# Head mixing on pieces of the TensorE array: four quarter products in place of one full product and three single-pass ones

## The chip, the cores and the metric

The kernel runs on one core of a Trainium2 chip. The metric is the device time of one execution in microseconds (us), lower is better. Before the change it is 1879.54 us, the median of 3 runs (1875.44 to 1880.68).

## The reference

```python
scores = (q @ k.T) / sqrt(64)                        # 8 batches, 12 heads, 448 tokens, head size 64
scores = einsum('bhij,hg->bgij', scores, w_pre)      # heads mixed before the softmax ("premix")
attn   = softmax(scores, axis=-1)                    # 1e-9 added to the sum
attn   = einsum('bhij,hg->bgij', attn, w_post)       # heads mixed after it ("mix")
x      = (attn @ v) as 3584 tokens x 768             # "values"
h      = x @ w_in                                    # 768 -> 2048
out    = (h - tanh(h)) @ w_out                       # 2048 -> 768
```

All inputs and the output are float32.

## The kernel before

The program has two stages on the time axis: attention up to about 931 us, then the feed-forward part, whose code the change leaves alone. In attention a batch's 448 query tokens are cut into blocks of 120, 120, 120 and 88. For a block, `scores` forms the products of two heads at a time on the two row halves of TensorE's array (fp32r, three products to each, line 475) and copies each head's 120x448 result from PSUM into the tile `s` (line 481, on ScalarE or VectorE).

To mix heads, 12 heads must lie on the partitions. So `gather` (line 496) moves, by a DMA from SBUF to SBUF, the 12 heads of ten tokens into one tile `t` of 120 partitions x 448 keys. A block has 12 (or 9) such groups of ten tokens, and the program's loop takes two groups at a place: 180 places in all. At place p:

1. `gather` of the two groups of place p+2, on SP's queue, and behind them up to six loads and stores that earlier places put into a list (`issue(6)`). Tiles of even groups have three buffers, those of odd groups two.
2. `premix(p)`: the even group in one float32 product with the block-diagonal 120x120 `wpre` (line 512); the odd group in three fp32r products (lines 515 to 517) from parts `th` and `tl` of its tile, which `split` made a place earlier on VectorE (line 504) and GpSimd (line 505).
3. `norm(p-1)`: reciprocals of the softmax sums, and `wpost` scaled by them into `wr` on ScalarE (line 545).
4. `expo(p)`: the row maximum on VectorE (line 527), exp with its sum on ScalarE (line 529).
5. What a plan puts into this place: `scores` of four heads of a later block, or half of the `values` of an earlier one (line 598, float32, on the two column halves of the array), transposes of q or k, loads.
6. `mix(p-1)`: for each group four float32 products of 112 keys each, with `e` as stationary operand and `wr` (120 columns) as moving one, into one PSUM tile `ps_o` with a single buffer (line 557). Its copy to `at` on ScalarE (line 566) is issued at the start of the next place.

Scores of heads 2hp and 2hp+1 go to ScalarE and VectorE for even hp, and both to ScalarE for odd hp, so three of four copies are ScalarE's. In the places beyond the fourth, steps of a conversion of the feed-forward weights (lines 80 to 104) are spread over VectorE, ScalarE and GpSimd.

The order on PE, ScalarE, VectorE, GpSimd and SP is the order of the code (`in_order`), so a waiting instruction holds what stands behind it on its engine. The loads of a batch's keys (`load_k`, three tiles of four heads, two buffers) are planned from the first place of the batch's predecessor's second block, less one, and their transposes (`prep_k`) two places after each load or later.

Of the kernel before, what the change touches and what calls it, by code (L numbers as in the profile page):

```python
# [148 lines left out]
def kernel_body(  # L149
# [21 lines left out]
    GP = GI * H  # L171
    starts = list(range(0, S, MT))
# [164 lines left out]
    with ExitStack() as st:  # L337
# [127 lines left out]
        def scores(i, hp, engines=None):  # L465

            b, m = blocks[i]
            n = sizes[m]
            if hp == 0:
                sts[i] = sp.tile([MT, H, S], F32, name="s", tag="s")  # L470
            (qh, ql), (kh, kl) = qbs[i], kks[b, hp // 2]
            pss = [ps_m.tile([P, 512], F32, name="ps_q", tag="ps_m") for _ in halves]
            for x, (qx, kx) in enumerate(((qh, kh), (qh, kl), (ql, kh))):
                for a, ps in zip(halves, pss):
                    nc.tensor.matmul(ps[:n, :S], qx[a, hp, :], kx[a, hp % 2], start=(x == 0), stop=(x == 2))  # L475

            def rest():

                two = engines or (nc.scalar.copy, nc.scalar.copy if hp % 2 else nc.vector.tensor_copy)
                for j, (eng, ps) in enumerate(zip(two, pss)):  # L480
                    eng(sts[i][:n, 2 * hp + j, :], ps[:n, :S])

            sooner.append(rest)
# [7 lines left out]
        tg, ts, te = {}, {}, {}  # L491

        def gather(t, eng=nc.sync):
            i, g = groups[t]
            x = gp.tile([GP, S], F32, name="t", tag=f"t{t % 2}", bufs=3 - t % 2)
            eng.dma_start(x[: rows[t], :], sts[i][tokens[t].start : tokens[t].stop : tokens[t].step])
            tg[t] = x

        def split(t, eng=nc.gpsimd):
            n = rows[t]  # L500
            x = tg.pop(t)
            th = gp.tile([GP, S], F32R, name="th", tag="th", bufs=2)
            tl = gp.tile([GP, S], F32R, name="tl", tag="tl", bufs=2)
            nc.vector.tensor_copy(th[:n, :], x[:n, :])  # L504
            eng.tensor_sub(tl[:n, :], x[:n, :], raw(th[:n, :]))  # L505
            ts[t] = (th, tl)

        def premix(p):

            pa, pb = [ps_p.tile([P, S], F32, name="ps_p", tag="ps_p") for _ in range(2)]  # L510
            n = rows[2 * p]
            nc.tensor.matmul(pa[:n, :], wpre[:n, :n], tg.pop(2 * p)[:n, :], start=True, stop=True)  # L512
            n = rows[2 * p + 1]
            th, tl = ts.pop(2 * p + 1)
            nc.tensor.matmul(pb[:n, :], wph[:n, :n], th[:n, :], start=True, stop=False)
            nc.tensor.matmul(pb[:n, :], wpl[:n, :n], th[:n, :], start=False, stop=False)
            nc.tensor.matmul(pb[:n, :], wph[:n, :n], tl[:n, :], start=False, stop=True)  # L517
            return pa, pb

        def expo(p, pss):  # L520
            zs = gp.tile([GP, 3, 2], F32, name="zs", tag="zs")
            es = []
            for j, ps in enumerate(pss):
                n = rows[2 * p + j]

                mx = gp.tile([GP, 1], F32, name="mx", tag="mx")
                nc.vector.tensor_reduce(out=mx[:n, :], in_=ps[:n, :], axis=AX.X, op=ALU.max, negate=True)  # L527
                e = gp.tile([GP, S], F32, name="e", tag="e", bufs=4)
                nc.scalar.activation(  # L529
                    e[:n, :], ps[:n, :], AF.Exp, bias=mx[:n, :], scale=1.0, accum_out=zs[:n, 0, j : j + 1]  # L530
                )
# [3 lines left out]
        def norm(p):  # L535
            zs = te[p][1]
            wr = gp.tile([GP, 2, P], F32, name="wr", tag="wr", bufs=2)[:, :, :GP]
            n0, n1 = rows[2 * p], rows[2 * p + 1]
            for j, n in enumerate((n0, n1)):

                nc.vector.tensor_scalar_add(zs[:n, 1, j : j + 1], zs[:n, 0, j : j + 1], 1e-9)
            for js, n in ((slice(0, 2), n0),) if n0 == n1 else ((slice(0, 1), n0), (slice(1, 2), n1)):
                nc.vector.reciprocal(zs[:n, 2, js], zs[:n, 1, js])
            for j, n in enumerate((n0, n1)):
                nc.scalar.mul(wr[:n, j, :], wpost[:n, :], zs[:n, 2, j : j + 1])  # L545
            te[p].append(wr)

        def mix(p):
            es, _, wr = te.pop(p)
            ps = ps_o.tile([P, 2, 512], F32, name="ps_o", tag="ps_o")  # L550
            for j, e in enumerate(es):
                i, g = groups[2 * p + j]
                n = rows[2 * p + j]
                if g == 0:
                    ats[i] = kp.tile([CP, NC, H, MT], F32, name="at", tag="at", bufs=2)
                for c in range(NC):
                    nc.tensor.matmul(  # L557
                        ps[:CP, j, c * GP : (c + 1) * GP], e[:n, c * CP : (c + 1) * CP], wr[:n, j, :],
                        start=True, stop=True,
                    )  # L560
# [90 lines left out]
        tmp_w = kp.tile([P, 2 * GP + 2 * H], F32, name="tmp_w", tag="at", bufs=2)  # L651
        w12 = tmp_w[:H, 2 * GP : 2 * GP + 2 * H].rearrange("p (w h) -> p w h", w=2)
# [11 lines left out]
        def scores_of(i, hq):  # L664
# [10 lines left out]
        repeat = tmp_w[:H, GP : 2 * GP]  # L675
        nc.gpsimd.memset(repeat, 0.0)
        nc.gpsimd.affine_select(
            out=repeat.rearrange("p (i h) -> p i h", i=GI), in_=repeat.rearrange("p (i h) -> p i h", i=GI),
            compare_op=ALU.not_equal, fill=1.0, base=0, pattern=[[0, GI], [-1, H]], channel_multiplier=1,
        )  # L680
        ps_w = bank()[:GP, : 2 * H].rearrange("p (w g) -> p w g", w=2)
        nc.tensor.matmul(ps_w.rearrange("p w g -> p (w g)"), repeat, w12.rearrange("p w g -> p (w g)"), start=True, stop=True)
        wpre, wpost = [cst.tile([GP, P], F32, name=x)[:, :GP] for x in ("wpre", "wpost")]
        pre_v = wpre.rearrange("p (i g) -> p i g", i=GI)
        post_v = wpost.rearrange("p (g i) -> p g i", i=GI)
        nc.vector.tensor_copy(pre_v, ps_w[:, 0, :].unsqueeze(1).to_broadcast([GP, GI, H]))
        nc.vector.tensor_copy(post_v, ps_w[:, 1, :].unsqueeze(2).to_broadcast([GP, H, GI]))
        for x, step in ((pre_v, [[H, GI], [0, H]]), (post_v, [[0, H], [H, GI]])):

            nc.gpsimd.affine_select(  # L690
                out=x, in_=x, compare_op=ALU.is_ge, fill=0.0, base=0, pattern=[[-a, n] for a, n in step],
                channel_multiplier=1,
            )
            nc.gpsimd.affine_select(
                out=x, in_=x, compare_op=ALU.is_ge, fill=0.0, base=H - 1, pattern=step, channel_multiplier=-1,
            )
# [23 lines left out]
        wph, wpl = [cst.tile([GP, P], F32R, name=x)[:, :GP] for x in ("wph", "wpl")]  # L720
        nc.vector.tensor_copy(wph, wpre)
        nc.vector.tensor_sub(wpl, wpre, raw(wph))
# [6 lines left out]
        split(1, nc.vector)  # L729
# [54 lines left out]
        for b in range(1, B):  # L784
            p, o, done = first[blocks.index((b - 1, 1))] // 2 - 1, 0, []
            for hq in range(3):
# [4 lines left out]
                o = max(p + 2, o + 1)  # L791
# [26 lines left out]
        for p in range(NPL + 3):  # L818
# [18 lines left out]
            if p + 1 < NPL:  # L837
                split(2 * p + 3)
# [97 lines left out]
```

## Time and profile before

| what | value |
|---|---|
| median of 3 runs | 1879.54 us |
| the profiled execution's own time | 1880.95 us |
| its span, first to last instruction | 1879.2 us |
| time outside the span | 1.75 us |
| mean granted TensorE clock | 0.998 |
| GpSimd busy | 451.9 us (24%) |
| line 505 (`tl`) on GpSimd | x179, 204.4 us |
| line 504 (`th`) on VectorE | x180, 82.4 us |
| line 545 (`wr`) on ScalarE | x360, 123.8 us |

A float32 product appears in the trace as two records of the same line, an fp32r product as one. A row of the timeline merges neighbours of the same line on one engine; its second number runs from the first start to the last end. PE's ends are modelled, so the starts of neighbours tell the rate.

### The profile page before, as it was taken

How to read it: one execution, taken by the hardware profiler on the slowest of the kernel's cores; microseconds unless marked ns; L12 is line 12 of the kernel's file. 1: busy time of each engine (PE TensorE's matmuls, PEld its weight loads, DVE VectorE, ACT ScalarE, POOL GpSimd, SP SyncE). 2: the span in 40 equal slices, each digit the busy share in tenths (PEclk: the TensorE clock that was granted, in tenths of full speed). 3: DMA queues.
4: the chain of work that ended last, by engine and by line, in shares of the span. 5: the costliest groups of instructions: out<-in, count | busy, mean ns of one | idle time of the engine just before them, and what ended most of it. 6: DMA issues, size and time to landing. Idle time of an engine off the chain costs nothing.

```text
span 1879.2 us, 35344 instructions
## 1 busy us (share of the span) xinstructions
PE 1851.1 (99%) x13150; PEld 1525.9 (81%) x13150; DVE 1184.7 (63%) x2457; ACT 1133.8 (60%) x2503; POOL 451.9 (24%) x401
## 2 busy tenths in 40 slices
PE   8999999999999999999999999999999999999998
PEld 6777887787878777877788888888888888888887
DVE  5676766767776676766456556556566566565555
ACT  5787887878888788788634443434434434433433
POOL 2344444444444345444201000000000000000000
PEclk9999999999999999999999999999999999999999
DMA  6667658676675757656565565665655655655651
GB/s 162 183 183 201 189 166 221 182 208 190 177 216 171 209 177 205 195 164 189 212 255 193 206 246 192 223 218 196 235 213 196 235 205 196 237 209 191 233 193 42
DMA packets 232795, 371.92 MB, mean 198 GB/s; under 512 B 98992, under 2 KB 207536, under 8 KB 218288
## 3 DMA queue, kind: packets, MB, share of 16 engines
q1 hardware_dynamic: 231740, 368.45, 60.5%
q8 instruction: 104, 1.70, 0.4%
q10 hardware_dynamic: 884, 1.22, 0.2%
q14 instruction: 67, 0.55, 0.1%
HBM read 245.37 MB, written 47.19 MB: 156 GB/s over the span
## 4 chain that ended last, share of the span: by engine, by line
PE 86%; DMA 6%; ACT 3%; DVE 2%; issue 2%; POOL 1%; SPq 0%; ACTq 0%; POOLq 0%; DVEq 0%
PE ps_o L557 13%; PE ps_h L256 8%; PE ps_h L260 8%; PE ps_h L255 8%; PE ps_m L598 7%; PE ps_p L512 6%; PE ps_q L475 6%; PE ya L303 5%; PE ya L300 5%; PE ya L301 5%; DMA t<-s 4%; PE yb L303 3%; PE yb L301 3%; PE yb L300 3%; PE ps_p L517 2%
## 5 line engine op out<-in xcount | busy, mean ns | idle before, releaser
L557 PEld LDWEIGHTS ps_o<-wr,e 120*112 120x112 f32 (+1 forms) x2880 | 307.2, 177 | 49.8 <-issue 30.1
L557 PE MATMUL ps_o<-wr,e 120*112 120x120 f32 (+1 forms) x2880 | 340.5, 271 | 4.1 <-ACT wr L545 4.1
L527 DVE TENSOR_REDUCE mx<-ps_p 120x1 f32<-120x448 f32 x360 | 218.6, 622 | 136.9 <-PE ps_p L512 136.7
L505 POOL TENSOR_TENSOR tl<-t,th 120x448 fp32r<-120x448 f32 x179 | 204.4, 1142 | 391.8 <-DVE th L504 221.5
L287 ACT CAST gh<-r 128x512 fp32r<-128x512 f32 x112 | 69.6, 621 | 373.3 <-DVE r L280 373.3
L256 PE MATMUL ps_h<-xl,w 128*128 128x512 f32 x672 | 263.2, 392 | 0.5 <-POOL pad L222 0.5
L255 PE MATMUL ps_h<-xh,w 128*128 128x512 f32 x672 | 262.8, 391 | 0.0
L529 ACT ACTIVATE e<-ps_p,mx 120x448 f32<-120x448 f32 x360 | 225.8, 636 | 36.7 <-DVE mx L527 36.1
L245 POOL TENSOR_TENSOR xl<-rx,xh 128x512 fp32r<-128x512 f32 x38 | 53.7, 1415 | 741.3 <-ACT xh L244 741.3
L566 ACT COPY at<-ps_o 112x960 f32<-112x960 f32 x156 | 154.5, 990 | 113.4 <-PE ps_o L557 112.5
L303 PE MATMUL ya<-w,gl 128*128 128x512 f32 x448 | 177.1, 395 | 0.7 <-DVE gl L288 0.7
L276 DVE SCALAR_TENSOR_TENSOR r<-qa,ps_h 128x512 f32<-128x512 f32 x112 | 77.0, 687 | 158.7 <-ACT t L273 158.7
L300 PE MATMUL ya<-w,gh 128*128 128x512 f32 x448 | 175.0, 391 | 1.3 <-ACT gh L287 1.3
L301 PE MATMUL ya<-w,gh 128*128 128x512 f32 x448 | 174.9, 390 | 0.0
L260 PE MATMUL ps_h<-xh,w 128*128 128x512 f32 x672 | 170.5, 389 | 0.0
L512 PE MATMUL ps_p<-t,wpre 120*120 120x448 f32 x360 | 165.7, 542 | 4.3 <-ACT e L529 3.5
L598 PE MATMUL ps_m<-at,vr 112*64 112x120 f32 (+1 forms) x3072 | 163.3, 263 | 1.9 <-ACT at L566 1.5
L598 PEld LDWEIGHTS ps_m<-at,vr 112*64 112x64 f32 x3072 | 149.7, 138 | 14.7 <-ACT at L566 3.7
L270 ACT ACTIVATE u<-ps_h 128x512 f32<-128x512 f32 x112 | 66.9, 597 | 149.2 <-PE ps_h L260 149.2
L260 PEld LDWEIGHTS ps_h<-xh,w 128*128 128x128 f32 x672 | 126.1, 188 | 26.2
L256 PEld LDWEIGHTS ps_h<-xl,w 128*128 128x128 f32 x672 | 126.6, 188 | 24.6 <-POOL pad L222 0.9
L255 PEld LDWEIGHTS ps_h<-xh,w 128*128 128x128 f32 x672 | 126.6, 188 | 22.9
(102 smaller groups left out, 3622.0 us busy)
## 6 DMA issues: line engine op xcount, KB each, us to landing
w<-ws SPq DMA_DIRECT2D x112, 1536.0 KB
t<-s SPq DMA_DIRECT2D x342, 210.0 KB
cr<-in_moe_w_in_dram SPq DMA_DIRECT2D x24, 512.0 KB
cr<-in_moe_w_out_dram SPq DMA_DIRECT2D x32, 384.0 KB
vr<-in_v_dram SPq DMA_DIRECT2D x24, 448.0 KB
kr<-in_k_dram SPq DMA_DIRECT2D x23, 448.0 KB
out_dram<-ob SPq DMA_DIRECT2D x24, 384.0 KB
qr<-in_q_dram SPq DMA_DIRECT2D x23, 360.0 KB
```

The lines of the kernel that those rows point to most:

```text
L255: nc.tensor.matmul(ph, wh[:, fs], xh, start=(c == 0), stop=False)
L256: nc.tensor.matmul(ph, wh[:, fs], xl, start=False, stop=False)
L260: nc.tensor.matmul(ph, wl[:, fs], xh, start=False, stop=(c == NK - 1))
L300: nc.tensor.matmul(y, gh[:, tok], wh[:, es], start=first, stop=False)
L301: nc.tensor.matmul(y, gh[:, tok], wl[:, es], start=False, stop=False)
L303: nc.tensor.matmul(y, gl[:, tok], wh[:, es], start=False, stop=last)
L505: eng.tensor_sub(tl[:n, :], x[:n, :], raw(th[:n, :]))
L512: nc.tensor.matmul(pa[:n, :], wpre[:n, :n], tg.pop(2 * p)[:n, :], start=True, stop=True)
L527: nc.vector.tensor_reduce(out=mx[:n, :], in_=ps[:n, :], axis=AX.X, op=ALU.max, negate=True)
L529: nc.scalar.activation(e[:n, :], ps[:n, :], AF.Exp, bias=mx[:n, :], scale=1.0, accum_out=zs[:n, 0, j : j + 1])
L557: nc.tensor.matmul(ps[:CP, j, c * GP : (c + 1) * GP], e[:n, c * CP : (c + 1) * CP], wr[:n, j, :], start=True, stop=True,)
L598: nc.tensor.matmul(pv[j * D : (j + 1) * D, r, :n], vt[:, j, c, :], ats[i][:, c, 2 * hp + j, :n], start=(c == 0), stop=(c == NC - 1),)
```

## The change

- `gather` moves a group in two DMAs of five tokens each (60 partitions): five tokens to partitions 0 to 59, the others to partitions 64 and up.
- `premix` makes four float32 products: group j and token half r, rows 64r and up of the array, columns 64j and up. Both groups' first halves land in one PSUM tile, both second halves in the other. `split`, `wph` and `wpl` are gone.
- `expo` and `norm` work on 128 partitions; `wr` has 60 columns in place of 120.
- `mix` makes 16 float32 products of 60 rows x 112 columns with 60 moving columns in place of 8 of 120 rows with 120 columns; group j lies on row half j, and the two alternate.
- of four score copies two go to ScalarE and two to VectorE.
- keys are loaded three places earlier, and transposed at the earliest four places after the load in place of two.

```diff
-        def split(t, eng=nc.gpsimd):
...
         def gather(t, eng=nc.sync):
             i, g = groups[t]
-            x = gp.tile([GP, S], F32, name="t", tag=f"t{t % 2}", bufs=3 - t % 2)
-            eng.dma_start(x[: rows[t], :], sts[i][tokens[t].start : tokens[t].stop : tokens[t].step])
+            x = gp.tile([P, S], F32, name="t", tag=f"t{t % 2}", bufs=3 - t % 2)
+            tok, n = tokens[t], half_rows(t)
+            src = lambda u: sts[i][u[0] : u[-1] + 1 : u.step]
+            for a, u in zip(halves, (tok[:GH], tok[GH:])):
+                eng.dma_start(x[a.start : a.start + H * len(u), :], src(u))
...
         def premix(p):
-            nc.tensor.matmul(pa[:n, :], wpre[:n, :n], tg.pop(2 * p)[:n, :], start=True, stop=True)
...
-            nc.tensor.matmul(pb[:n, :], wph[:n, :n], th[:n, :], start=True, stop=False)
-            nc.tensor.matmul(pb[:n, :], wpl[:n, :n], th[:n, :], start=False, stop=False)
-            nc.tensor.matmul(pb[:n, :], wph[:n, :n], tl[:n, :], start=False, stop=True)
+            for j, to in enumerate(halves):
+                for r, (a, ps) in enumerate(zip(halves, pss)):
+                    k = slice(a.start, a.start + H * half_rows(2 * p + j)[r])
+                    nc.tensor.matmul(ps[to, :], wpre[k, :], ts[j][k, :], start=True, stop=True)
...
         def mix(p):
-                for c in range(NC):
-                    nc.tensor.matmul(
-                        ps[:CP, j, c * GP : (c + 1) * GP], e[:n, c * CP : (c + 1) * CP], wr[:n, j, :],
+            for r, e in enumerate(es):
+                for c in range(NC):
+                    for j, a in enumerate(halves):
+                        k = slice(a.start, a.start + H * half_rows(2 * p + j)[r])
+                        nc.tensor.matmul(
+                            ps[:CP, j, c * GP : (c + 1) * GP].rearrange("p (h i) -> p h i", i=GI)[:, :, r * GH : (r + 1) * GH],
+                            e[k, c * CP : (c + 1) * CP], wr[k, r, :],
...
-                two = engines or (nc.scalar.copy, nc.scalar.copy if hp % 2 else nc.vector.tensor_copy)
+                two = engines or (nc.scalar.copy, nc.vector.tensor_copy)
...
-            p, o, done = first[blocks.index((b - 1, 1))] // 2 - 1, 0, []
+            p, o, done = first[blocks.index((b - 1, 1))] // 2 - 4, 0, []
...
-                o = max(p + 2, o + 1)
+                o = max(p + 4, o + 1)
```

The order on PE, before, over a place with scores and the mix ahead of it (`ps_o` is mix, `ps_p` premix, `ps_q` scores):

```order
L557 MATMUL ps_o<-wr,e 112x120 x8
L512 MATMUL ps_p<-t,wpre 120x448
L515 MATMUL ps_p<-th,wph 120x448
L516 MATMUL ps_p<-th,wpl 120x448
L517 MATMUL ps_p<-tl,wph 120x448
L475 MATMUL ps_q<-kk,qh 88x448 x4
L475 MATMUL ps_q<-kk,ql 88x448 x2
L475 MATMUL ps_q<-kk,qh 88x448 x4
L475 MATMUL ps_q<-kk,ql 88x448 x2
L557 MATMUL ps_o<-wr,e 112x120 x8
```

The same place on PE, now:

```order
L554 MATMUL ps_o<-wr,e 112x12x5 x16
L516 MATMUL ps_p<-t,wpre 64x448 x4
L477 MATMUL ps_q<-kk,qh 88x448 x4
L477 MATMUL ps_q<-kk,ql 88x448 x2
L477 MATMUL ps_q<-kk,qh 88x448 x4
L477 MATMUL ps_q<-kk,ql 88x448 x2
L554 MATMUL ps_o<-wr,e 112x12x5 x16
```

Nothing changes places on PE: four products stand where four stood, sixteen where eight stood.

SP's queue at a batch's end, before (`t<-s` is a gather, `kr` keys, `vr` values, `xs` the attention's result, `cr` and `ws` the weight conversion):

```order
L367 DMA xs_57<-x 768x1x208
L496 DMA t<-s 120x1x448 x2
L367 DMA qr<-in_q_dram 88x12x64
L367 DMA vr<-in_v_dram 112x4x256
L367 DMA kr<-in_k_dram 112x16x64
L367 DMA ws_65<-cs 128x384
L367 DMA ws_65<-cl 128x384
L496 DMA t<-s 120x1x448 x2
L367 DMA vr<-in_v_dram 112x4x256
L367 DMA kr<-in_k_dram 112x16x64
```

and now:

```order
L505 DMA t<-s 60x1x448 x8
L369 DMA kr<-in_k_dram 112x16x64
L369 DMA ws_65<-cs 512x1x128
L369 DMA ws_65<-cl 512x1x128
L505 DMA t<-s 60x1x448 x4
L369 DMA kr<-in_k_dram 112x16x64
L369 DMA cr<-in_moe_w_out_dram 128x768
L505 DMA t<-s 60x1x448 x4
L369 DMA vr<-in_v_dram 112x4x256
L369 DMA xs_57<-x 768x1x208
L505 DMA t<-s 60x1x448 x4
```

The first two loads of keys moved ahead of the store of `xs` and away from the loads of values, and each place has four gathers.

What the gathers of two places wait for on SP, before (`PE` and `Pool` are those engines' use of the buffer that the gather overwrites, `DMAHW` an earlier transfer that must have landed):

```order
L496 DMA t<-s 120x1x448 [waits DMAHW2_49,PE_49]
L496 DMA t<-s 120x1x448 [waits DMAHW3_49,Pool_49]
L367 DMA kr<-in_k_dram 112x16x64 [waits DMAHW4_49]
L496 DMA t<-s 120x1x448 [waits DMAHW5_49,PE_49]
L496 DMA t<-s 120x1x448 [waits DMAHW6_49,DMAHW0_49,Pool_49]
```

and now:

```order
L505 DMA t<-s 60x1x448 [waits DMAHW4_49,DVE_49,Activation_49]
L505 DMA t<-s 60x1x448 [waits DMAHW5_49]
L505 DMA t<-s 60x1x448 [waits DMAHW6_49,PE_49]
L505 DMA t<-s 60x1x448 [waits DMAHW7_49]
L369 DMA kr<-in_k_dram 112x16x64 [waits DMAHW0_49]
L505 DMA t<-s 60x1x448 [waits DMAHW1_49]
L505 DMA t<-s 60x1x448 [waits DMAHW2_49]
L505 DMA t<-s 60x1x448 [waits DMAHW3_49,PE_49]
```

The odd group's gather waited for GpSimd, which a place earlier had made `tl` from that buffer; it now waits for PE, that is for the premix of its own place.

More of the change, by code (lines that the diff above doesn't have):

```diff
@@ L673, in kernel_body @@
         flush()
[L675 removed]
+        repeat = tmp_w[:H, :P]
         nc.gpsimd.memset(repeat, 0.0)
[L677 to L681, printed above, removed]
[L682 removed]
@@ L683, in kernel_body @@
[L683 to L696, printed above, removed]
+        for a in halves:
+            nc.gpsimd.affine_select(
+                out=repeat[:, a][:, :HP].rearrange("p (i h) -> p i h", i=GH),
+                in_=repeat[:, a][:, :HP].rearrange("p (i h) -> p i h", i=GH),
+                compare_op=ALU.not_equal, fill=1.0, base=0, pattern=[[0, GH], [-1, H]], channel_multiplier=1,
+            )
@@ L699, in kernel_body @@
+        for w, x in enumerate((wpre, wpost)):
+            nc.gpsimd.memset(x[:, HP:], 0.0)
+            nc.vector.tensor_add(x[:, :HP], both[:, w, 0], both[:, w, 1])
         busy(3, ps_b)
```

88 lines of the change are left out of this document (46 added, 42 removed).

## The prediction

> **What bounds the kernel now.** I read the page first, then the engines' busy time over the steady part of attention.
>
> ```profile
> PE 1851.1 (99%) x13150; PEld 1525.9 (81%) x13150; DVE 1184.7 (63%) x2457; ACT 1133.8 (60%) x2503; POOL 451.9 (24%) x401
> ...
> 94.00:940.00 846.00, 833.43 (x7707) 667.96 (x7703) 584.64 (x1528) 688.11 (x1705) 373.30 (x331) 1.00 0.65 192
> 940.00:1879.00 939.00, 932.19 (x4791) 790.31 (x4789) 545.62 (x792) 382.34 (x648) 51.84 (x38) 1.00 0.57 206
> ```
>
> In attention PE is busy 833 of 846 us, VectorE (third number) 585, ScalarE (fourth) 688, GpSimd 373; the granted clock is full. So a microsecond that leaves PE is a microsecond gained until ScalarE, at 81%, is next. What the places cost stands in PE's timeline: one with scores, one with only premix and mix, and one with values.
>
> ```profile
> 391.71 0.92 PE L512 MATMUL ps_p<-t,wpre 120*120 120x448 f32 x2
> ...
> 392.67 0.37 PE L516 MATMUL ps_p<-th,wpl 120*120 120x448 f32 x1
> 392.87 0.36 PE L517 MATMUL ps_p<-tl,wph 120*120 120x448 f32 x1
> 393.16 0.67 PE L475 MATMUL ps_q<-kk,qh 64*120 64x448 f32 x4
> ...
> 394.27 0.37 PE L475 MATMUL ps_q<-kk,ql 64*120 64x448 f32 x2
> 394.56 1.90 PE L557 MATMUL ps_o<-wr,e 120*112 120x120 f32 x16
> 396.30 0.92 PE L512 MATMUL ps_p<-t,wpre 120*120 120x448 f32 x2
> ...
> 397.81 1.90 PE L557 MATMUL ps_o<-wr,e 120*112 120x120 f32 x16
> 399.55 0.54 PE L512 MATMUL ps_p<-t,wpre 120*120 120x448 f32 x1
> ```
> ```profile
> 365.77 0.92 PE L512 MATMUL ps_p<-t,wpre 108*108 108x448 f32 x2
> ...
> 367.24 2.68 PE L598 MATMUL ps_m<-at,vr 112*64 112x120 f32 x48
> 369.85 1.90 PE L557 MATMUL ps_o<-wr,e 120*112 120x120 f32 x16
> 371.58 0.54 PE L512 MATMUL ps_p<-t,wpre 120*120 120x448 f32 x1
> ```
>
> From start to start, the scores place is premix 1.45, scores 1.40, mix 1.74, together 4.59 us; the values place 1.47 + 2.61 + 1.73 = 5.81; the bare place 3.25. How many there are follows from the groups:
>
> ```profile
> L512 PE MATMUL ps_p<-t,wpre 120*120 120x448 f32 x360 | 165.7, 542 | 4.3 <-ACT e L529 3.5 <-DMA t<-s 0.8
> L598 PE MATMUL ps_m<-at,vr 112*64 112x120 f32 (+1 forms) x3072 | 163.3, 263 | 1.9 <-ACT at L566 1.5 <-ACT at L573 0.3
> L475 PE MATMUL ps_q<-kk,qh 64*120 64x448 f32 (+1 forms) x768 | 119.3, 386 | 1.1 <-ACT kk L426 0.4 <-ACT qh L454 0.3 <-DVE zs L541 0.2
> ```
>
> Premix has two records per float32 product, so 360 are 180 places. Scores have eight `qh` records in a place: 96 sets, 4 of them ahead of the loop, leave 92 places. Values have 48 in a place: 64 sets, the last two behind the last place, leave 62. The other 26 I treat as bare.
>
> **Premix.** Of a float32 product the second record starts 0.38 us after the first (0.92 from first start to last end, 0.54 each), so one product is 0.76. All turns on how many of the four quarter products run at once. Halves do: the 48 values records take 2.61 us, 0.054 each, where mix, with as many moving columns in the same type, takes 1.74/16 = 0.109. That could still come of one product's second record running beside the next one's first. What speaks for more is the first tenth of a microsecond of values, cut out of the timeline:
>
> ```profile
> 367.23 0.20 PEld L598 LDWEIGHTS ps_m<-at,vr 112*64 112x64 f32 x4 [0.31 <-ACT wr L545]
> 367.24 0.32 PE L598 MATMUL ps_m<-at,vr 112*64 112x120 f32 x2
> ...
> L598 PE MATMUL ps_m<-at,vr x48: 266/266/317, 367.2 to 369.7; 112*64 112x120 f32 x48
> ```
>
> Two records are under way from the start and both end within 0.32 us, the longest single one being 0.317: the second did not wait behind the first. Since both records of a product use the same half, the second must be the other half's, taken ahead of the first half's second record. If it looks past three neighbours as it does past one, all four quarters run together: two turns of 0.38 = 0.76. The other end, quarters one after another, is 3.04. No row shows four at once; I take 0.76, as both directions of halving show it by twos. [...]
>
> Around it: 0.05 for its own weights of 64 columns (317 − 266 ns above), and a gap where the shape of the array changes. The last score product starts at 394.27, streams 0.20 (as 392.67 to 392.87) and mix starts 0.09 later. Premix to scores or values has this gap before and after; mix to premix gets it newly; scores to mix, both on row halves now, loses it. Premix: 1.45 (1.47) becomes 0.05 + 0.76 + 0.09 = 0.90.
>
> **Mix.** 32 records instead of 16, each of 60 moving columns, half of 0.1 us. The weights keep 112 columns, and their loads may now be what sets the pace:
>
> ```profile
> L557 PE MATMUL ps_o<-wr,e x16: 266/266/357, 394.6 to 396.2; 120*112 120x120 f32 x16
> ...
> 393.16 0.28 PEld L475 LDWEIGHTS ps_q<-kk,qh 64*120 64x120 f32 x4 [0.31 <-ACT at L566]
> ...
> L475 PEld LDWEIGHTS ps_q<-kk,qh x8: 176/178/179, 393.2 to 393.9; 64*120 64x120 f32 x8
> ```
>
> The first mix product waits 357 − 266 = 91 ns for weights. Row halves load side by side: four loads of 0.178 each are over in 0.28. So 16 pairs at 0.096 (91 ns and a few to hand over) make 1.54. One after another they would make 2.98. [...] Behind scores, mix needs neither gap nor exposed weights: 1.54, and 0.09 into premix, 1.63. Behind values the weights are exposed: 1.72.
>
> **The places' sums.** Scores place: 0.90 + 1.31 + 1.63 = 3.84 (scores without its closing gap), 0.75 less, × 92 = 69 us. Values place: 0.90 + 2.61 + 1.72 = 5.23, 0.58 less, × 62 = 36 us. The bare place does not follow PE, as ScalarE's timeline shows:
>
> ```profile
> 391.91 0.98 ACT L566 COPY at<-ps_o 112x960 f32<-112x960 f32 x1 [2.01 <-PE ps_o L557]
> 392.79 0.67 ACT L545 ACTIVATE wr<-wpost,zs 120x120 f32<-120x120 f32 x2
> 393.38 0.63 ACT L529 ACTIVATE e<-ps_p,mx 120x448 f32<-120x448 f32 x1
> ...
> 394.61 1.40 ACT L481 COPY s<-ps_q 120x448 f32<-120x448 f32 x3
> 396.50 0.98 ACT L566 COPY at<-ps_o 112x960 f32<-112x960 f32 x1 [0.49 <-PE ps_o L557]
> 397.37 0.68 ACT L545 ACTIVATE wr<-wpost,zs 120x120 f32<-120x120 f32 x2
> ```
>
> From the end of mix (396.30) 0.20 to the copy, 0.87 to `wr`, 0.44 to the next mix at 397.81, and that mix: 3.25. This circle stays, with `wr` of 60 columns some 0.04 shorter and mix at 1.63: 3.10, 0.15 less, × 26 = 4 us. Together 109 us.
>
> **What takes some of it back.** ScalarE in the scores place: copy 0.88, `wr` 0.59, exp 1.23, three score copies 1.40, 4.10; with two copies 3.6. The weight conversion comes on top:
>
> ```profile
> L85 ACT ACTIVATE cr<-cr 128x384 f32<-128x384 int32 (+1 forms) x56 | 35.4, 634 | 0.0
> L82 ACT ACTIVATE cm<-cm 128x384 f32<-128x384 f32 (+1 forms) x56 | 33.1, 594 | 0.0
> L102 ACT CAST cs<-cm 128x384 fp32r<-128x384 f32 (+1 forms) x56 | 32.2, 578 | 1.2 <-POOL cm L98 1.1
> ...
> L481 DVE COPY s<-ps_q 120x448 f32<-120x448 f32 (+1 forms) x100 | 62.0, 621 | 16.8 <-PE ps_q L475 16.3 <-DMA ws<-cs 0.4
> L504 DVE CAST th<-t 120x448 fp32r<-120x448 f32 (+1 forms) x180 | 82.4, 458 | 50.2 <-DMA t<-s 50.2
> ```
>
> 100.7 us over 164 places is 0.61 a place. Spread evenly it makes 4.2 against PE's 3.84, 0.37 too much; before, it made 4.71 against 4.59, and the neighbouring values places took it. Bounds: 0 and 0.37 × 92 = 34 us; I take half, 17. VectorE gets 92 more score copies (92 × 0.62 = 57 us) and loses 82 of `th`: no cost. GpSimd loses 204 us that nobody waited long for: no gain.
>
> The gathers. Until now a late odd tile stopped VectorE, a place ahead of its premix (the first row, from 94 to 930 us); now it stops PE:
>
> ```profile
> DVE th L504 <- DMA t<-s: 45.3, 22, 5.6
> ...
> 362.12 1.73 SPq L496 DMA_DIRECT2D t<-s  x2
> 363.90 0.52 SPq L367 DMA_DIRECT2D qr<-in_q_dram  x1
> ```
>
> The odd gather now waits on SP for premix(p) to free its buffer, and behind it wait the loads and stores of its place and the next place's even gathers. It has two places less premix, some 7 us, till it is needed. A gather issue is 0.87 here and two make 1.73; four halves are between 1.7 and 3.5 a place, and the 1.4 other issues 0.5 each: SP keeps within 4.2 us. The late tiles stood at 45 us in 22 waits, part of them hidden under values. Bounds 0 and 45; I take 15.
>
> The keys. Their loads leave the crowd at the batch's end; transposes waited for them 3.9 us in all:
>
> ```profile
> PE ps_m L415 <- DMA kr<-in_k_dram: 3.9, 3, 1.4
> ```
>
> I count 4, between 0 and 8, since the crowd also delays gathers. Setup (eight small masks for four, no `wph`) is within 2 us either way, and the feed-forward part is untouched. Sum: −109 + 17 + 15 − 4 = −81. The profiled execution took 1880.95 us, 1.4 more than the median of the runs, so 1800.
>
> **The rivals.** *Three turns.* If PE looks past one pair only, two quarters run their second records beside the first ones of the other two: 3 × 0.38 = 1.14. Scores place 4.22, now at ScalarE's 4.2, values 5.61, bare 3.10: 34 + 12 + 4 = 50 less, with gathers and keys 39: 1842. For it: no row shows a look past two.
>
> *Taking turns.* Slower: records start strictly in program order, first and second of a quarter, so that only one second and one first ever overlap: five turns, 1.90. Scores place 4.98, values 6.37, bare 3.76 (now PE's): 36 + 35 + 13 = 84 more, 1965. Against it is the pair at 367.24. [...] It decides from premix of 1.37 on (109/180 = 0.61 above 0.76), less than four turns. Mix loads that run one after another would come to the same side: 1.44 × 180 = 259 more than forecast, some 2060; the four loads in 0.28 speak against them.
>
> *Transfers become the bound.* At 192 GB/s over 846 us, attention moves 162 MB; in 80 us less that is 212 GB/s. The feed-forward part moves 206 on the average, so there is room, but little is shown. If gathers come late at every batch's end, with the full 45 us on PE and more from crowding, 1830 to 1875; at worst the gain is gone.
>
> **How the numbers follow.** Forecast (1775 to 1830 by the bounds above) 0.62; three turns 0.12; transfers 0.12, of it 0.03 with no change left; taking turns 0.13; no effect for another reason 0.01. 0.3% (5.6 us) is about what a measurement of this kernel can tell from no change. So faster 0.83, same 0.04, slower 0.13. The range 1770 to 1870 holds the forecast, three turns and most of the transfers' case.
>
> **What would show it.** Right: from premix's first start to the scores' first some 0.9 us, 16 mix pairs in 1.6, scores places near 4.0, ScalarE over 85% busy in attention, GpSimd at half. Wrong: premix starts 0.38 apart by ones or twos; mix near 3; PE waits "DMA t<-s" of more than 45 us; attention ending after 900 us.

## The result, and the profile after

| | median us | lowest to highest | to before, 95% interval |
|---|---|---|---|
| before | 1877.49 | 1875.19 to 1880.68 (4 runs) | |
| after | 1945.32 | 1941.28 to 1950.49 (4 runs) | 1.0362 [1.033, 1.0393] |

Slower, by 68 us, where 80 us less was forecast. The stages first (length, then busy time of PE, weight loads, VectorE, ScalarE and GpSimd with their instructions, the granted clock, the DMA engines' share, GB/s): attention, and the feed-forward part. That part takes what it took before: from the end of the last mix to the end of the span it is 942 us in both profiles.

```profile
94.00:986.00 892.00, 845.35 (x10824) 610.66 (x10822) 533.80 (x1431) 639.57 (x1605) 183.84 (x164) 0.95 0.60 179
1008.00:1939.00 931.00, 924.89 (x4685) 785.11 (x4683) 542.22 (x789) 379.90 (x644) 52.32 (x36) 1.00 0.58 208
```

So the loss is in attention, whose last premix starts 55 us later (the two profiled executions are 60 us apart), with a granted clock of 0.95 in place of 1.00 and with less moved in a second (179 GB/s against 192). PE's timeline, an undisturbed place with values and one with scores:

```profile
378.30 2.68 PE L596 MATMUL ps_m<-at,vr 112*64 112x120 f32 x48
380.91 1.78 PE L554 MATMUL ps_o<-wr,e 60*112 60x60 f32 x32
...
411.96 0.98 PE L516 MATMUL ps_p<-t,wpre 60*64 60x448 f32 x8
412.87 0.66 PE L477 MATMUL ps_q<-kk,qh 64*120 64x448 f32 x4
...
414.18 1.69 PE L554 MATMUL ps_o<-wr,e 60*112 60x60 f32 x32
415.80 3.56 PE L516 MATMUL ps_p<-t,wpre 60*64 60x448 f32 x8
```

From start to start premix is 0.91, scores 1.31, mix 1.62: 3.84, the forecast to the hundredth; values are 2.61. So PE's part came out as predicted. But the next premix, at 415.80, takes 3.56 for the same eight records: there a place loses 2.6 us. Its four products start 0.63, 1.02 and 0.95 us after one another in place of all within 0.02 us, as their halves land. What PE and its weight loads waited for in attention (engine, tile and line, releaser: us in total, times, longest):

```profile
PE ps_m L596 <- DMA vr<-in_v_dram: 19.0, 7, 4.3
...
PE ps_p L516 <- DMA t<-s: 6.2, 15, 0.7
```
```profile
PEld ps_p L516 <- DMA t<-s: 57.0, 82, 1.4
...
PEld ps_m L596 <- DMA vr<-in_v_dram: 13.6, 5, 4.7
```

PE and its weight loads often wait for the same thing at the same time, so the rows of the two don't add up. The gathers are late 82 times, by a little each, and the values' loads seldom, but by much. Both go through SP. Its gather issues, first before, then after (count, nanoseconds least/median/most, first and last start):

```profile
L496 SPq DMA_DIRECT2D t<-s x326: 768/787/5422, 97.3 to 917.9; - x163
```
```profile
L505 SPq DMA_DIRECT2D t<-s x621: 665/745/5652, 93.9 to 937.6; - x156
```

Half a gather costs SP 0.745 us, a whole one 0.787. Between 94 and 900 us SP's instructions, some of them waiting, cover 532 of 806 us before and 702 after, and its pauses of over 0.3 us shrink from 230 us to 53. What a late load then costs on PE:

```profile
300.09 0.98 PE L417 MATMUL ps_m<-ident,kr 112*128 112x112 f32 x8
303.54 1.86 PE L596 MATMUL ps_m<-at,vr 112*64 112x120 f32 x32 [2.46 <-DMA vr<-in_v_dram]
309.64 1.87 PE L596 MATMUL ps_m<-at,vr 112*64 112x120 f32 x16 [4.25 <-DMA vr<-in_v_dram]
311.44 3.25 PE L554 MATMUL ps_o<-wr,e 60*112 60x60 f32 x32
314.62 1.77 PE L516 MATMUL ps_p<-t,wpre 60*64 60x448 f32 x8
```

After waits of 2.46 and 4.25 us the mix takes 3.25 and the premix 1.77 in place of 1.69 and 0.98: the array runs at half clock and pays the wait a second time (the granted clock is 0.50 from 309 to 318 us). Over all of attention, 5% of 892 us is 45 us, with the rounding of that column 40 to 49; this is an estimate and a ceiling, since PE also waited in some of that time. In this place the clock falls 3.3 us into the wait of 4.25. Elsewhere it falls after less: the trace has eleven stretches at half clock between 94 and 986 us, 89 us together, and before ten of them PE's longest wait in some 9 us is 0.5 to 2.3 us. In the 9 us before seven of the ten, weight loads waited for gathers, 0.6 to 3.1 us in all. That gathers late by a little each cost clock too is argued from these rows; no run shows it apart.

### The profile page after: what moved, and what is told of

Its sections match the earlier page's. It is cut to its first block, busy times and chain, and to the rows that moved or that the text cites. A ratio compares the mean times of both kernels' runs of the same rounds, so it can differ in the third digit from the quotient of the medians.

```text
span 1939.3 us, 42060 instructions
## 1 busy us (share of the span) xinstructions
PE 1869.2 (96%) x16570; PEld 1470.3 (76%) x16570; DVE 1131.8 (58%) x2362; ACT 1089.0 (56%) x2411; POOL 250.2 (13%) x229
## 4 chain that ended last, share of the span: by engine, by line
PE 78%; DMA 11%; SPq 4%; ACT 3%; DVE 3%; issue 1%; POOL 0%; ACTq 0%; DVEq 0%; POOLq 0%
PE ps_o L554 10%; PE ps_p L516 8%; PE ps_h L257 8%; PE ps_h L258 8%; PE ps_h L262 8%; DMA t<-s 7%; PE ps_m L596 6%; PE ya L305 5%; PE ya L302 5%; PE ya L303 5%; PE ps_q L477 4%; SPq L505 3%; PE yb L305 3%; PE yb L303 3%; PE yb L302 3%
## 5 line engine op out<-in xcount | busy, mean ns | idle before, releaser
L554 PEld LDWEIGHTS ps_o<-wr,e 60*112 60x112 f32 (+1 forms) x5760 | 315.6, 180 | 56.1 <-ACT wr L539 41.4
L554 PE MATMUL ps_o<-wr,e 60*112 60x60 f32 (+1 forms) x5760 | 325.7, 264 | 23.3 <-ACT wr L539 23.1
L525 DVE TENSOR_REDUCE mx<-ps_p 128x1 f32<-128x448 f32 x360 | 211.2, 618 | 197.0 <-PE ps_p L516 195.9
L516 PE MATMUL ps_p<-t,wpre 60*64 60x448 f32 (+1 forms) x1440 | 271.9, 580 | 11.1 <-DMA t<-s 8.5
L527 ACT ACTIVATE e<-ps_p,mx 128x448 f32<-128x448 f32 x360 | 225.8, 634 | 68.6 <-DVE mx L525 66.7
L596 PE MATMUL ps_m<-at,vr 112*64 112x120 f32 (+1 forms) x3072 | 172.8, 271 | 25.2 <-DMA vr<-in_v_dram 19.0
L596 PEld LDWEIGHTS ps_m<-at,vr 112*64 112x64 f32 x3072 | 157.3, 143 | 50.0 <-DMA vr<-in_v_dram 13.6
L277 DVE TENSOR_SCALAR far<-u 128x512 f32<-128x512 f32 x112 | 47.8, 426 | 143.6 <-ACT u L272 135.9
```

The costliest lines, as they stand in the source:

```text
L516: nc.tensor.matmul(ps[to, :], wpre[k, :], ts[j][k, :], start=True, stop=True)
L525: nc.vector.tensor_reduce(out=mx, in_=ps, axis=AX.X, op=ALU.max, negate=True)
L527: nc.scalar.activation(e, ps, AF.Exp, bias=mx, scale=1.0, accum_out=zs[:, 0, r : r + 1])
L554: nc.tensor.matmul(ps[:CP, j, c * GP : (c + 1) * GP].rearrange("p (h i) -> p h i", i=GI)[:, :, r * GH : (r + 1) * GH], e[k, c * CP : (c + ...
L596: nc.tensor.matmul(pv[j * D : (j + 1) * D, r, :n], vt[:, j, c, :], ats[i][:, c, 2 * hp + j, :n], start=(c == 0), stop=(c == NC - 1),)
```

## The experiments

Theory A, formed from these rows: SP's issue time is the bound. Its rivals: (B) too short a lead of the odd groups' gathers, (C) places that are now too short for transfers and clock, and (D) halves that move worse than whole gathers. D came up only after the run with the cut alone, below.

**Is it the lead, or SP's load?** A third buffer for odd groups:

```diff
-            x = gp.tile([P, S], F32, name="t", tag=f"t{t % 2}", bufs=3 - t % 2)
+            x = gp.tile([P, S], F32, name="t", tag=f"t{t % 2}", bufs=3)
```

> The changed kernel with three buffers for odd group tiles too, so that SP need not wait for the premix of the same place before it issues the odd gathers. Theory A (SP's issue time: four gathers of 0.745 us and 1.4 other issues a place, some 4 us against PE's 3.85 to 5.2): the queue stays as full, 1925 to 1950 us. Theory B (the lead: SP is held by PE at each odd gather, and everything behind comes a place later than before the change): most waits for gathers and values go, 1800 to 1850 us.

Measured 1931.66, 1.028 [1.0255, 1.0304]: 14 us less than after. The lead alone is not it. All loads and stores of the list on GpSimd's queue:

```diff
-                    send(x, nc.sync)
+                    send(x, nc.gpsimd)
```

> The changed kernel with the loads and stores of the loop's list (keys, queries, values, the weight conversion, the attention's result) issued on GpSimd's queue, the gathers left on SP. Theory A: SP has 3.0 us of gathers a place and keeps up, 1800 to 1860 us, if GpSimd's issues cost it no more than the some 75% it sits idle. Theory B: SP is still held by PE at odd gathers, but fewer issues stand behind it: 1880 to 1930 us.

Measured 1970.24, 1.0491 [1.0473, 1.0508]: slower than after, outside what was expected. With the loads gone SP now waits much, for the gathers' buffers and for gathers under way, and the gathers come later still:

```profile
SPq L505 <- PE ps_q L477: 151.6, 56, 5.5
SPq L505 <- PE ps_p L516: 98.4, 66, 4.4
SPq L505 <- DMA t<-s: 95.8, 61, 5.0
```
```profile
PEld ps_p L516 <- DMA t<-s: 88.9, 60, 4.4
```

An engine with 346 us of such waits is not short of issue time. This speaks against A as the whole cause. The second halves on GpSimd's queue:

```diff
-                eng.dma_start(x[a.start : a.start + H * len(u), :], src(u))
+                (eng if a.start == 0 else nc.gpsimd).dma_start(x[a.start : a.start + H * len(u), :], src(u))
```

> The changed kernel with the second half of every gather issued on GpSimd's queue. Theory A: SP has 1.5 us of gathers and 0.9 of others a place, 1800 to 1840 us. Theory B: both queues are held by PE at the odd group, and only SP's own length is relieved: 1860 to 1920 us.

Measured 1903.66, 1.0129 [1.0106, 1.0152]: 42 us less. The time is above A's range and inside B's. The run halves SP's gathers, but it also moves half of the rows by another queue, where the trace has them in packets of 5376 B, three rows each (SP's have one; in the run with this queue and three odd buffers, below, packets of 512 B to 2 KB are 21408 fewer than in after, those of 2 to 8 KB 7136 more), so it doesn't tell A from D.

**The cut alone, in the kernel before.** Each gather as two DMAs of five tokens, the products as they were:

```diff
-            eng.dma_start(x[: rows[t], :], sts[i][tokens[t].start : tokens[t].stop : tokens[t].step])
+            tok = tokens[t]
+            for a, u in ((0, tok[: GI // 2]), (H * (GI // 2), tok[GI // 2 :])):
+                eng.dma_start(x[a : a + H * len(u), :], sts[i][u[0] : u[-1] + 1 : u.step])
```

> The kernel before with every gather issued as two DMAs of five tokens, nothing else changed. Theory A: SP goes from some 2.6 to 4.1 us a place of 5.0 on the average; it falls behind in places with several loads, 1890 to 1930 us. Theory B: SP keeps its lead of a place and the kernel its time, 1875 to 1885 us.

Measured 1963.47, 1.0446 [1.043, 1.0462]: 84 us more by the cut alone, more than any theory had. Then the gather whole, and behind it a DMA of twelve rows of 256 B that nobody reads:

```diff
+            y = gp.tile([H, D], F32, name="extra", tag="extra", bufs=2)
+            eng.dma_start(y, sts[i][tokens[t].start : tokens[t].start + 1, :, :D])
```

> The kernel before with one more DMA behind each gather, 12 rows of 256 bytes that nobody reads: the count of SP's issues as after the change, the gathers whole. Theory A: if a small issue between tiles costs SP 0.6 us or more, 1930 to 1965 us, as with split gathers. Rival D (the halves themselves are the trouble: 60 rows from five partitions move worse than 120 from ten): 1878 to 1890 us.

Measured 1897.81, 1.0105 [1.0085, 1.0125]: 20 us more, between what A and D had expected. The issues in the two kernels, first the small DMA's, then the halves':

```profile
L498 SPq DMA_DIRECT2D extra<-s x329: 729/743/1351, 93.6 to 932.0; - x165
```
```profile
L498 SPq DMA_DIRECT2D t<-s x604: 657/742/4406, 94.1 to 935.8; - x151
```

As many issues, each at the same 0.74 us, and 66 us between them. So a second issue for each gather explains some 20 of the 84. What is left over must be in how the halves move, and the DMA view shows a difference there, in short windows in which nothing else moves: one whole gather in before (a window of 1.0 us), the two halves of one in the kernel with the cut (1.9 us). The first line has the busy share of the 16 engines in 40 slices, the last the packets and the share over the window.

```profile
DMA  0037397193393773791973973933937917934000
...
DMA packets 130, 0.22 MB, mean 215 GB/s; under 512 B 10, under 2 KB 130, under 8 KB 130
...
q1 hardware_dynamic: 130, 0.22, 56.1%
```
```profile
DMA  0312412412412412412522412412412421421100
...
DMA packets 130, 0.22 MB, mean 113 GB/s; under 512 B 10, under 2 KB 130, under 8 KB 130
...
q1 hardware_dynamic: 130, 0.22, 29.5%
```

The packets are the same 120 rows and ten small writes. The whole gather takes 0.93 us, with 0.561 x 16 x 1.0 / 0.93 = 9.7 engines busy; the halves take 1.77 us, with 0.295 x 16 x 1.9 / 1.77 = 5.1 busy. The rows of one token go one behind the other on one engine, 12 x 0.071 = 0.85 us: ten tokens on ten engines, five on five. The second half's rows start 6 ns after the first half's small writes: on the same five engines, though eleven others stand idle. The trace has no engine numbers; this is read from the rhythm, in which each of five streams takes up its next row 6 ns after its small write. The semaphores agree: the median half in the changed kernel gets five late updates, a whole gather before ten. In a crowd (issues less than 0.95 us apart, 94 to 900 us) halves land 0.86 us apart in the median, where SP issues them 0.79 apart. That halves queue behind each other on five engines all through attention is argued from this and from the one window.

**D against A, by cutting the other way.** As many DMAs, rows and bytes, but each half takes six heads of all ten tokens; first in the kernel before:

```diff
-            for a, u in ((0, tok[: GI // 2]), (H * (GI // 2), tok[GI // 2 :])):
-                eng.dma_start(x[a : a + H * len(u), :], sts[i][u[0] : u[-1] + 1 : u.step])
+            for a, u in ((0, slice(0, H // 2)), (rows[t] // 2, slice(H // 2, H))):
+                eng.dma_start(x[a : a + rows[t] // 2, :], sts[i][tok[0] : tok[-1] + 1 : tok.step, u])
```

> The kernel before with each gather as two DMAs of 60 rows, cut by heads instead of by tokens (the numbers of the attention are not the reference's, since the rows stand in another order). Cut by tokens it took 1963.5; with a small second DMA of the same issue time, 1897.8. Theory A: 1945 to 1970, as by tokens. Theory D: 1885 to 1910, as with the small one.

Measured 1891.54, 1.0065 [1.0044, 1.0086]: 72 us less than cut by tokens. VectorE's waits for odd gathers, cut by tokens and then by heads:

```profile
DVE th L506 <- DMA t<-s: 198.5, 98, 7.0
```
```profile
DVE th L506 <- DMA t<-s: 48.3, 27, 5.6
```

Then the same cut in the changed kernel:

```diff
-            n = rows[t] // H
-            return (GH, n - GH)
+            n = rows[t] // 2
+            return (n, n)
...
-            src = lambda u: sts[i][u[0] : u[-1] + 1 : u.step]
-            for a, u in zip(halves, (tok[:GH], tok[GH:])):
-                eng.dma_start(x[a.start : a.start + H * len(u), :], src(u))
+            src = lambda u: sts[i][tok[0] : tok[-1] + 1 : tok.step, u]
+            for a, u in zip(halves, (slice(0, H // 2), slice(H // 2, H))):
+                eng.dma_start(x[a.start : a.start + n[0], :], src(u))
...
```

The premix and the mix take their rows by the new `half_rows`.

> The changed kernel with its two DMAs a gather cut by heads instead of by tokens: the first takes heads 0 to 5 of all ten tokens, the second heads 6 to 11, each 60 rows of 1792 B as before. The products and everything else are the same, so the numbers of the attention are not the reference's: the time alone is read. Theory A (SP's issue time of two DMAs at 0.745 us each is what is paid): as many issues, so 1930 to 1955 us. Theory D (the rows of one token go one behind the other, 12 x 0.071 = 0.85 us, so that a half of five tokens takes as long to move as a whole gather of ten, and two halves twice as long): ten tokens side by side with six rows each take 0.43, and the time falls to 1860 to 1900, with the halves landing as fast as they are issued. Both at work would lie between.

Measured 1850.75, 0.9847 [0.9824, 0.9869]: 95 us less than after. D had the way right and was too careful, since this is below its range. Three views of it: SP's issues, the weight loads' wait for gathers, and a lone half in a window of 0.6 us:

```profile
L505 SPq DMA_DIRECT2D t<-s x656: 761/767/2723, 93.2 to 881.5; - x164
...
  PEld ps_p L516: 7.4, 18
```
```profile
DMA packets 70, 0.11 MB, mean 179 GB/s; under 512 B 10, under 2 KB 70, under 8 KB 70
...
q1 hardware_dynamic: 70, 0.11, 47.3%
```

SP issues as much as in after, a little dearer even (0.767), and the weight loads' wait for gathers falls from 57.0 to 7.4. A half takes 0.51 us with 0.473 x 16 x 0.6 / 0.51 = 8.9 engines busy; its ten small writes, one to a stream in the windows above, tell of ten. Counted on PE, from each premix's first start to the next other product, the premixes from 94 us on (166 and 165) take 112 us more than 0.91 each in after, and 35 us more cut by heads: most of the 95 us lies there, half clock included. The two cuts differ in the number of engines and in the number of source partitions alike, so the runs show that five in place of ten is the cause, and only the rows above that it is engines.

**The products without the cut.** One DMA to partitions 0 to 119:

```diff
-            for a, u in zip(halves, (tok[:GH], tok[GH:])):
-                eng.dma_start(x[a.start : a.start + H * len(u), :], src(u))
+            eng.dma_start(x[: rows[t], :], src(tok))
...
-                    k = slice(a.start, a.start + H * half_rows(2 * p + j)[r])
+                    k = slice(a.start, a.start + (H * GH if r == 0 else last_rows(2 * p + j)))
```

`last_rows` is `rows[t] - D`: the second quarters take the 56 rows from partition 64 on, and four rows of each full group are left out.

> The changed kernel with each group gathered by one DMA to partitions 0 to 119, as before the change; the second half's rows then lie four partitions low, and its quarter products take the rows there are, so the numbers of those tokens are not the reference's, while every other instruction and size stays. Theory A (SP's issues, 0.745 us for half a gather where a whole one takes 0.79): SP goes back to 2.6 us a place, the PE saving shows, 1785 to 1835 us. Rival C (it is the shorter places themselves: transfers and clock can't follow): 1880 to 1930 us.

Measured 1823.0, 0.971 [0.9688, 0.9733]. The places are as short here as in after, so C is not the cause. The same with all rows in their place: ten tokens go to partitions 4 to 123, so that the sixth begins at partition 64. The first quarter takes rows 0 to 63, with weights moved down by four rows and zeros above them, and fixed buffers whose first four rows are cleared once.

```diff
+        tbuf = [cst.tile([P, S], F32, name=f"t{n}") for n in range(5)]
...
-            x = gp.tile([P, S], F32, name="t", tag=f"t{t % 2}", bufs=3 - t % 2)
+            x = tbuf[3 + t // 2 % 2 if t % 2 else t // 2 % 3]
...
-            for a, u in zip(halves, (tok[:GH], tok[GH:])):
-                eng.dma_start(x[a.start : a.start + H * len(u), :], src(u))
+            eng.dma_start(x[D - HP : D - HP + rows[t], :], src(tok))
...
-                    k = slice(a.start, a.start + H * half_rows(2 * p + j)[r])
-                    nc.tensor.matmul(ps[to, :], wpre[k, :], ts[j][k, :], start=True, stop=True)
+                    k = slice(a.start, a.start + (H * half_rows(2 * p + j)[r] if r else D))
+                    nc.tensor.matmul(ps[to, :], wsh[k, :], ts[j][k, :], start=True, stop=True)
```

> The changed kernel with one DMA a gather: ten tokens go to partitions 4 to 123, so that the sixth token begins at partition 64 and the quarter products find both halves where they want them; the first half's products take rows 0 to 63, with zeros in the first four rows of the weights and of five fixed buffers. Nothing is left out. If the cut of the gather alone made the change slow (theory D with A), 1810 to 1835, as the run with one whole gather (1823.0). If that run was fast because its second half took fewer rows, or the longer first half costs, 1840 or more.

Measured 2069.6, 1.1022 [1.1008, 1.1036], a miss of the experiment's own: the program has the gather for place p+2 ahead of premix(p), so with two fixed buffers premix(p) reads the odd group of place p+2, and waits for it. Its time says nothing of the cut, nor does that of the run with the keys besides (2083.1, expectation below), only what a lead of nothing costs.

> One DMA a gather, with the keys loaded and transposed as before the change. The prediction gave the earlier loads 4 us, between 0 and 8: so 0 to 8 us more than the first run of these four. If earlier keys push out the values' loads, as PE's 19 us of waits for values in the changed kernel hint, no more or some us less.

With premix written ahead of the gathers of its place, so that SP waits for it as in after:

> One DMA a gather to partitions 4 to 123, two odd buffers, premix written ahead of the gathers of its place, so that the odd gather waits for it as in the changed kernel. If the third buffer is what the run of 1791.8 has over the one with one whole gather (1823.0), 1815 to 1830; if the fixed buffers or the rows did it, 1792 to 1805.

Measured 1821.73, 0.9699 [0.9678, 0.9721], with the one above it (1823.0). So the change with a whole gather is 57 us faster than before, and with two halves by tokens 68 slower. That the two runs agree, though only one has the order of the code changed, speaks against an effect of that order. With a third buffer for odd groups, the order of the code as it was:

> As the run before it, with three buffers for odd groups. If odd gathers still come late for want of lead, 10 to 20 us less than that run; if, with one DMA a gather, SP has room, within 5 us of it.

Measured 1791.76, 0.9541 [0.9528, 0.9555]: 30 us less by the buffer, twice what it brought in after. PE's waits with two odd buffers, then with three:

```profile
PE ps_m L597 <- DMA vr<-in_v_dram: 13.4, 8, 3.7
...
PE ps_p L517 <- DMA t<-s: 1.7, 3, 0.9
```
```profile
PE ps_m L597 <- DMA vr<-in_v_dram: 1.7, 2, 1.5
...
PE ps_p L517 <- DMA t<-s: 0.3, 1, 0.3
```

Not the gathers were late with two, but the values, whose loads stand on SP behind a gather that waits for its buffer. That is argued from these rows; the run shows that the buffer takes the waits away. They are 11.7 of the 18.5 us between the two profiled executions; no row here shows where the rest of the 30 us goes.

**The loads' places.** In that kernel, the keys as before the change:

```diff
-            p, o, done = first[blocks.index((b - 1, 1))] // 2 - 4, 0, []
+            p, o, done = first[blocks.index((b - 1, 1))] // 2 - 1, 0, []
...
-                o = max(p + 4, o + 1)
+                o = max(p + 2, o + 1)
```

> One DMA a gather to partitions 4 to 123, three odd buffers, as in the run of 1791.8, with the keys loaded and transposed as before the change. By the prediction's term the earlier keys bring 4 us, between 0 and 8: 1792 to 1800. If they cost more than they bring, by holding the values' loads, below 1792.

Measured 1813.93, 0.9666 [0.9641, 0.9692]: 22 us more, so the earlier keys bring 22 there. The same edit in after:

> The changed kernel with the keys' loads and transposes planned as before the change. If the earlier loads help a late queue: 1955 to 1985 us; if they only shift the crowd ahead of the values, which PE waited for 33 us: 1915 to 1940 us; if neither: 1940 to 1950 us.

Measured 1950.85, 1.0383 [1.0368, 1.0399], 5 us more, which the intervals don't tell from none. PE's waits for keys in these two:

```profile
PE ps_m L417 <- DMA kr<-in_k_dram: 15.6, 5, 5.5
```
```profile
PE ps_m L417 <- DMA kr<-in_k_dram: 43.3, 6, 11.7
```

In after the early keys take away 43 us of waits, and values are late instead: 19.0 us of PE's waits there, 0.9 with the keys as before. And the values' loads one place earlier (`p0 + 3 + hq` for `p0 + 4 + hq`) in the kernel of 1791.76:

> As the run before it, with the values' loads a place earlier. With one whole gather PE still waited 11.8 us for values. If they are late issues, 5 to 15 us less than the run before; if the packets are full at a batch's end, within 4 us.

Measured 1798.8, 0.9588 [0.9566, 0.961]: 7 us more, a miss. There was nothing left to gain (1.7 us of waits); why it costs stays open.

**Halves on GpSimd's queue.** Here, too, the rows on GpSimd's queue go by threes (the packets counted above are the first of these runs'), so who issues and how the rows move change together. Second halves there and three odd buffers:

> Second halves of gathers on GpSimd's queue, and three buffers for odd tiles. With SP relieved, the lead can matter: theory A with the lead as second cause: 1830 to 1880 us. If the lead doesn't matter even then: 1895 to 1910 us, as with the queue alone (1903.7).

Measured 1860.53, 0.9893 [0.9874, 0.9912], 71 us less than three odd buffers with all halves on SP's queue (1931.66). With the values a place earlier:

> Second halves on GpSimd's queue, three odd buffers as in the run of 1860.5, and the values' loads a place earlier. PE waited there 18.4 us for values. If those waits are only late issues, 1838 to 1855 us; if the values are late because the queue and the packets are full, 1855 to 1875, and other waits take their place.

Measured 1865.21, 0.9923 [0.9901, 0.9945]. With all halves but the first four groups' there:

> As the run before it, with both halves of every gather but the first four on GpSimd's queue, so that SP issues no gathers at all. Theory A (issue time on SP): GpSimd would issue 712 x 0.6 = 427 us beside its 181 us of other work, SP under 300: 1820 to 1860. Theory D, or GpSimd's work held behind waiting gathers: 1860 to 1960.

Measured 1872.57, 0.996 [0.9946, 0.9975]. After the first four groups SP issues no gathers here, and it is 74 us above the whole gather on SP's queue with three buffers and the values as early (1798.8). So relief of SP is not needed for the gain, and by this queue it does not bring it; how much of the 71 us is relief and how much another way of moving, no run tells.

## Why the prediction was wrong

- *Premix, mix and the places' sums.* Right for two kinds of place of three: premix 0.91 for 0.90, mix 1.62 for 1.63, the scores place 3.84 for 3.84, the values place 5.24 for 5.23 (median, kernel of 1791.8). Not for the bare place: there it is 3.35 in the median, where 3.10 was forecast and 3.25 stood before, some 7 us over the 26 counted. All four quarters run together (four starts within 0.02 us); neither three turns nor taking turns came. That the time lies near the 1965 of taking turns is chance: its mechanism isn't there.
- *What they are worth.* With a whole gather and three odd buffers the kernel takes 1791.8 where 1800 was forecast: the 109 us and what was taken off are about of the right size there. That they meet to 8 us is in part luck, since the keys brought 22 for 4, the bare places nothing for 4, and the third buffer was in no term.
- *The gathers*, the step that failed: "four halves are between 1.7 and 3.5 a place, and the 1.4 other issues 0.5 each: SP keeps within 4.2 us". Two things were wrong in it. A half costs SP 0.745, inside that range, so four are 3.0 and with the others 3.7 of a place of 3.84: there is no room left, and the 4.2 should have been held against the 3.84 forecast just above it. By the cut by heads against the whole gather, a second DMA for each gather costs 1850.75 − 1821.73 = 29 us; that this is its issue is argued, from the 20 us of the small DMA. And the step priced only the issue: how long a half takes to move is put at nothing in it. It moves in the whole gather's time, so four in a row on five engines, an estimate from the two halves' 1.77 us and the 0.86 us between landings, take 3.4 to 3.6 us of a place of 3.84; how much of these engines the other loads need no run shows. By the cut by tokens against the one by heads that is 1945.32 − 1850.75 = 95 us. The row 130 packets in 0.93 us was in the trace of before; ten busy engines of sixteen could have been read from it.
- *Late tiles*, 15 of "bounds 0 and 45": the bound came from a kernel with whole gathers and was no bound. Weight loads wait 57.0 us for gathers in after, the premixes take 112 us more than 0.91 each, and the half clock, up to 45 us in all, is nowhere in the prediction. Two of its own signs of being wrong came: waits for `t<-s` above 45 us, and an attention that ends after 900 us.
- *Two odd buffers.* Their wait for premix was seen and held to be covered by two places of lead. It cost 30 us with whole gathers, as far as it was followed through the values behind it.
- *Keys*, 4 between 0 and 8: 22 where gathers are whole, and 5 in after, which is not clear of none.
- *ScalarE*, 17: not measured apart. In the kernel of 1791.8 places with scores, counted from premix to premix from 94 us on, have a mean of 3.98 where the forecast had 3.84 + 17/92 = 4.02. But their median is 3.86, so a few long places make the mean, and the agreement doesn't show the term. The nearest row is PE's wait for `wr`, 13.2 us there and 4.1 before.
- *The range.* "1775 to 1830 by the bounds above" is narrower than its bounds: added up they give 1764 to 1851.
- *Transfers become the bound* was the right rival with the wrong price. It went by the mean GB/s over sixteen engines ("at worst the gain is gone"); by the rows above the bound was five of them, and the time passed through no change to 68 us more.

The account now, from runs: 1877.5 before; −57 for the change with a whole gather; +29 for a second DMA for each gather; +95 for halves on five engines in place of ten. These are differences along one row of runs, so they must come to the 1945.3 measured; the sum proves nothing by itself. What carries it is the cut by heads, which has as many DMAs, rows and bytes as the cut by tokens.

## What to carry to other kernels

When a DMA is cut in two, price both the issue and the move: here the issue stayed at 0.74 us and the move at 0.9, so the cut doubled both. Count the engines a transfer runs on from a lone one in the trace, and look for a layout that keeps it whole before paying for two: moved by four partitions, the same rows serve the quarter products, and with a third buffer the kernel is 4.6% faster than before. A queue that has room before a change is to be held against the shorter place after it.

## What was not expected of the hardware

- SP's issue of a gather hardly depends on its size: 0.787 us for 120 rows of 1792 B, 0.745 for 60, 0.743 for 12 rows of 256 B.
- A DMA of 60 rows took as long as one of 120 (0.9 us) when its source had five partitions, and 0.51 when it had ten.
- Four 60-row by 64-column float32 products run at once: the eight records of premix take 0.98 us from first start to last end, where one product alone took 0.92 before.
- Half clock followed short waits as well: before ten of the eleven half-clock stretches in attention after the change, no wait of PE in some 9 us was longer than 2.3 us.
